# A scan and two expert layers on one core: scatters spaced by steps, one more tile table, later chunks, eight tiles half by half

## The chip, the core and the metric

The kernel runs on one core of one Trainium2 chip. The core has five engines with a queue of instructions each: TensorE (PE; its weight loads are listed as PEld), VectorE (DVE), ScalarE (ACT), GpSimd (POOL) and SyncE (SP), which issues DMAs only. Sixteen DMA engines serve the DMAs of all of them. The metric is the device time of the program in microseconds, the median of several runs.

## The reference

Tokens are 2 x 5056 rows of 256 numbers. A gated scan runs along each sequence; then each token goes through one of eight experts, picked by the largest logit, and the result through a second layer of eight experts with a gate of its own.

```
sig = 1 / (1 + exp(-f_logit)); f = lb + (1 - lb) * sig
h[t] = f[t] * h[t-1] + (1 - f[t]) * x[t]            # y, N = 10112 rows of D = 256
# layer 1: logits = normed(y) @ normed(emb).T / tau;  layer 2: logits = x @ w_gate
e = argmax(logits); g = softmax(logits)[e]
out[n] = g * (relu(x[n] @ w1[e]) @ w2[e])           # w1: 256 x 1024, w2: 1024 x 256, E = 8
```

## The kernel before

**Blocks, chunks, tiles, units.** The 10112 rows are 79 blocks of 128, and a chunk is two blocks (40 chunks, numbered from 0). A chunk is loaded transposed (`p_load`, 512 KB), gated (`p_gate`: tanh on ScalarE, the rest on ScalarE or GpSimd), scanned along the row on VectorE (`p_scan`, L492), transposed on TensorE with its logits (`p_mm`, L507 and L509), scaled and split into a high and a low half of 16 bits (`p_hi`, `p_lo`), and ranked by expert. Two chunks share a row tile of four blocks. GpSimd then scatters each block's 128 rows by an indirect DMA into the table X[0] in DRAM (`p_put`, L638), where every expert has a region of its own.

A tile is 128 rows of one expert. Which expert a tile belongs to and where it starts is computed on the core (`checkpoint`): once the first 16, 32, 48, 64 blocks are scattered, and at the end, a table is made of the tiles that are full by then in any case (9, 16, 16, 16 and the rest). SyncE reads the table into registers and loads a tile with a transposing DMA (`t_load`, L755) and its gate values (L762).

A unit is half an expert for one tile: 512 of the 1024 hidden columns. It has 24 matmuls of 128 columns into PSUM (`mm1`, L780), a Relu on ScalarE and its low part on VectorE (`evac`, L788 and L187, the tile hT) and 12 matmuls of 256 columns (`mm2`, L802). A layer has 83 tiles or 166 units in the main order, 332 units for both; three more tiles of each layer run only if they hold rows. A tile's two units normally follow each other. The first 4 tiles of the kernel (`g0`, group 1) and the last 21 of layer 1 and first 21 of layer 2 (`swap`, group 2) go half by half: all tiles with the first half of the experts, then all with the second, so that the weights of one half can be loaded meanwhile. Such a tile is loaded twice, keeps a partial sum (`o_partial`, L806) and adds it on VectorE (`o_sum`, L195).

**Layer 1 to layer 2.** A finished tile of layer 1 is summed, scaled, split, transposed again (`m_turn`: by DMA for the tiles of group 0 below number 48, on TensorE, L868, for the others), gets its logits, expert and slot (`m_logits` to `m_slot`), and its rows are scattered into X[1] (L948, two scatters for a pair of tiles). Layer 2 reads its tiles from X[1] and scatters its results to the output (L970).

**Weights.** Each expert's half of W1 and of W2 is loaded as 512 KB of 32-bit numbers and split into a high part (`w_hi`, ScalarE) and a low part (`w_lo`, VectorE; four of the first sixteen on TensorE and ScalarE). There are 32 such items for each layer.

**Order.** The order is written out by hand as numbered steps. Step i >= 0 issues unit i; the prologue starts at step -31. Each piece of work is entered at a step with a priority: `at(step, prio, function)`. A chunk c starts at step s0[c]: from -29 in twos, chunk 8 at -9 (`hold`), in twos up to chunk 17 and in fours behind it (`rates`). Its parts follow at fixed distances (`p`): load -2, scan 0, transposes 2, its row tile's four scatters 7 to 10, the checkpoint 7. `m`, `md` and `mg` hold the same for a finished tile (normal, turned by DMA, half by half). Up to step 16 only SyncE keeps this order (`man0`), the other engines' instructions are placed by the framework's scheduler; from step 17 (`mans`) TensorE, SyncE, GpSimd and ScalarE keep it too (`man`). DMAs of chunks and weights go to SyncE ahead of step -6 (`spto`), to ScalarE's queue behind it. Chunks 0 to 7 lie in the buffers of the second half of W2 (`alias`); chunks from 8 on, row tiles and some others share a pool of six buffers (tag `q`). A tile is loaded up to six units ahead (`pre`), into four buffers.

Of the kernel before, what the change touches and what calls it, by code (L numbers as in the profile page):

```python
# [11 lines left out]
I32 = mybir.dt.int32  # L12
# [12 lines left out]

CFG = {'cps': (16, 32, 48, 64),
 'g0': 4,
 'swap': 21,
# [9 lines left out]
 'gdve': 0,  # L38
 'wpe': (4, 0),
 'yg': (0, 0),  # L40
 'man0': ('SP',),
# [6 lines left out]
 'mans': 17,  # L48
 'xtn': 48,
 'md': {'turn': (3, 58),  # L50
        'logits': (8, 3),
# [5 lines left out]
        'up': (12, 45),  # L57
        'done': (12, 57)},
 'hiv': (2,),
# [4 lines left out]
 'sc': (0, 26),  # L64
 'w1': (-8, 0.8),
 'w1s': (20, 0.8),
# [58 lines left out]
def scan_moe_moe_kernel(ctx, tc, xf, emb, cst, tmp, w1a, w2a, w1b, w2b, out, seq, cfg=CFG):  # L125
# [6 lines left out]
    CT = 2  # L132
# [500 lines left out]
    def p_put(q, rows):  # L633
        p = pq[q]
        for i in rows:
            if i >= p["g"]:
                return
            x_write(0, G.indirect_dma_start(out=X[0], out_offset=IndirectOffsetOnAxis(ap=p["sl"][:, i, 0:1], axis=0),  # L638
                                            in_=p["row"][:, i, :].bitcast(I32), in_offset=None, bounds_check=BOUND,
                                            oob_is_err=False))  # L640
            yield
# [72 lines left out]

    ring = {}

    wreg = [T.alloc_register(f"wa{i}") for i in range(16)]
# [66 lines left out]
    def evac(t, h):  # L784
        hps = t.pop("hps")
        hT = hp.tile([P, 8, P], F16, name="hT", tag="hT", bufs=LAG + 2)
        hh = hT.rearrange("p (a c) q -> p a (c q)", a=2)
        A.activation(out=hh[:, 0], in_=hps, func=ACTF.Relu)  # L788
        stt(V, hh[:, 1], hps, 0.0, hh[:, 0], ALU.max, ALU.subtract)
        t["hT", h] = hT  # L790
# [143 lines left out]
    def m_slot(d):  # L934
        g = len(d["t"])
        pz = d["er"]
        assert ranked[1] == 1
        ranked[1] = 0
        tt(V, pz, RK[:, G4:G4 + g], d["oh"][:, 0:g], ALU.mult)
        yield  # L940
        slf = sm.tile([P, CT, 1], F32, name="tslf", tag="tslf")[:, 0:g]
        V.tensor_reduce(out=slf, in_=pz, axis=AX.X, op=ALU.add)
        yield
        sl = sm.tile([P, CT, 1], I32, name="tsl", tag="tsl")[:, 0:g]
        stt(V, sl, slf, 1.0, d["inv"].unsqueeze(2), ALU.mult, ALU.add)
        yield
        for i in range(len(d["t"])):
            x_write(1, G.indirect_dma_start(out=X[1], out_offset=IndirectOffsetOnAxis(ap=sl[:, i, 0:1], axis=0),  # L948
                                            in_=d["row"][:, i].bitcast(I32), in_offset=None, bounds_check=BOUND,
                                            oob_is_err=False))  # L950
            yield

# [94 lines left out]
    for c in range(NCH):  # L1047
        if c == cfg["hold"][0]:
            s = cfg["hold"][1]
        s0[c] = int(s)  # L1050
        s += next(r for n, r in cfg["rates"] if c < n)
    first = min(s0.values())
    for c in range(NCH):
# [8 lines left out]
        if 2 <= c < cfg["alias"]:  # L1062
            at(first - 2 + (c - 2) // 2, 2, p_load, c)
        elif c >= 2:
            pa("load", p_load, c)
        for name, fn in (("gate", p_gate), ("scan", p_scan), ("mm", p_mm), ("sq", p_sq), ("pow", p_pow), ("hi", p_hi), ("lo", p_lo)):
            pa(name, fn, c)
        if c % 2 or c == NCH - 1:
# [7 lines left out]
            else:  # L1076
                for j in range(G4):
                    at(b + j, prio, p_put, q, (j,))

# [110 lines left out]
    def fin_unit(u, i):  # L1190
# [4 lines left out]
        elif h == 1:  # L1195
# [11 lines left out]
            if t["pi"] == len(d["t"]) - 1:  # L1207
                for name, fn in (("scale", m_scale), ("split", m_split), ("turn", m_turn), ("turn2", m_turn2),
                                 ("logits", m_logits), ("top", m_top), ("exp", m_exp), ("rank", m_rank),
                                 ("gat", m_gat), ("slot", m_slot), ("up", m_up), ("done", done_pair)):  # L1210
                    ma(name, fn, d)

    def drain(g):
# [10 lines left out]
    def last_tiles(m):  # L1224
# [22 lines left out]
        with tc.If(n > tl[0]["j"], label=f"tail{m}"):  # L1247
            kept[0] = {}
            assert ranked[1] == 0
            for d in [t["pair"] for t in tl if t["pi"] == 0]:  # L1250
# [9 lines left out]
                for fn in (m_scale, m_split, m_turn, m_turn2, m_logits, m_top, m_exp, m_rank, m_gat, m_slot, m_up):  # L1260
                    drain(fn(d))
                routed[0] += len(d["t"])
            kept[0] = None
# [129 lines left out]
```

## Time and profile before

| what | us |
|---|---|
| median of 3 runs | 1064.48 (1055.07 to 1067.7) |
| the profiled execution | 1052.77 |
| its span, first to last instruction | 1050.9 |
| TensorE busy | 996.1 (95%) |
| VectorE, ScalarE, GpSimd busy | 602.3, 529.2, 407.8 |
| mean granted TensorE clock | 0.985 |

The span is one execution; its own time stands beside it, and it lies below the three timed runs. Busy times are unions of an engine's instructions. A busy TensorE can be waiting inside a matmul or run at half its clock, so its share alone does not tell how near it is to its best.

### The profile page before, as it was taken

How to read it: one execution, taken by the hardware profiler on the slowest of the kernel's cores; microseconds unless marked ns; L12 is line 12 of the kernel's file. 1: busy time of each engine (PE TensorE's matmuls, PEld its weight loads, DVE VectorE, ACT ScalarE, POOL GpSimd, SP SyncE). 2: the span in 40 equal slices, each digit the busy share in tenths (PEclk: the TensorE clock that was granted, in tenths of full speed). 3: DMA queues.
4: the chain of work that ended last, by engine and by line, in shares of the span. 5: the costliest groups of instructions: out<-in, count | busy, mean ns of one | idle time of the engine just before them, and what ended most of it. 6: DMA issues, size and time to landing. Idle time of an engine off the chain costs nothing. (4 is left out here: it accounts for less than half of the span.)

```text
span 1050.9 us, 36737 instructions
## 1 busy us (share of the span) xinstructions
PE 996.1 (95%) x13267; PEld 932.6 (89%) x13267; DVE 602.3 (57%) x1927; ACT 529.2 (50%) x1301; POOL 407.8 (39%) x666
## 2 busy tenths in 40 slices
PE   5557999999999999999999999999999999999997
PEld 4436889999999999999998999999999999999997
DVE  7988877787778777665449778443222222222221
ACT  6978555665655565665346466443333333333332
POOL 5834645666666565332002550243222222222222
PEclk9967999999999999999999999999999999999999
DMA  9798436777677673875479699653322222222220
GB/s 352 244 342 209 132 59 120 144 136 130 124 127 127 152 125 94 195 196 149 62 170 205 123 197 267 117 103 72 52 52 53 52 53 48 45 50 44 47 51 31
DMA packets 195612, 132.69 MB, mean 126 GB/s; under 512 B 169601, under 2 KB 172558, under 8 KB 195440
## 3 DMA queue, kind: packets, MB, share of 16 engines
q1 hardware_dynamic: 172384, 60.18, 29.7%
q10 hardware_dynamic: 11200, 38.62, 14.7%
q0 software_dynamic: 11856, 31.51, 11.7%
q8 instruction: 118, 1.93, 0.8%
q14 instruction: 54, 0.44, 0.2%
HBM read 58.89 MB, written 38.85 MB: 93 GB/s over the span
## 5 line engine op out<-in xcount | busy, mean ns | idle before, releaser
L780 PE MATMUL hps<-xT,W 128*128 128x128 f16 x7968 | 504.9, 220 | 6.9 <-DVE hT L187 3.1
L802 PE MATMUL ops<-W,hT 128*128 x3984 | 489.3, 272 | 1.6 <-ACT acc L806 0.9
L780 PEld LDWEIGHTS <-W 128*128 x7968 | 475.6, 98 | 16.0 <-issue 6.3
L187 DVE SCALAR_TENSOR_TENSOR hT<-hps,hT 128x512 f16<-128x512 f32 x332 | 228.6, 688 | 318.4 <-ACT hT L788 315.7
L802 PEld LDWEIGHTS <-hT 128*128 128x128 f16 x3984 | 374.3, 98 | 41.4 <-issue 2.0
L788 ACT ACTIVATE hT<-hps 128x512 f16<-128x512 f32 x332 | 198.0, 596 | 303.2 <-PE hps L780 284.0
L970 POOL DMA_INDIRECT out<-osum,ti x83 | 81.1, 977 | 291.4 <-ACT osum L966 189.5
L948 POOL DMA_INDIRECT X<-trow,tsl x83 | 97.1, 1170 | 53.2 <-DVE tsl L187 18.0
L638 POOL DMA_INDIRECT X<-row,sl x79 | 92.8, 1174 | 55.1 <-issue 37.7
L966 ACT ACTIVATE osum<-ops,exr 128x256 f32<-128x256 f32 x62 | 29.3, 473 | 47.0 <-PE ops L802 44.8
L195 POOL TENSOR_TENSOR lf<-exr,us 128x2 f32<-128x2 f32 (+1 forms) x42 | 9.7, 231 | 102.6 <-DMA W<-WD 44.0
L187 DVE SCALAR_TENSOR_TENSOR W<-ws,W 128x1024 f16<-128x1024 f32 x34 | 41.5, 1220 | 8.7 <-ACT W L373 8.7
L373 ACT ACTIVATE W<-ws 128x1024 f16<-128x1024 f32 x35 | 37.1, 1060 | 12.5 <-DMA ws<-w2b 8.6
L825 ACT ACTIVATE trow<-osum 128x256 f16<-128x256 f32 x83 | 34.9, 420 | 16.0 <-DMA X<-trow,tsl 7.6
L492 DVE TENSOR_TENSOR_SCAN xf<-xf 128x256 f32<-128x256 f32 (+3 forms) x64 | 42.8, 710 | 0.1
L507 PE MATMUL yt<-cs,xf 128*128 128x128 f32 x126 | 28.3, 303 | 15.2 <-DVE xf L492 10.2
L814 ACT ACTIVATE osum<-ops 128x256 f32<-128x256 f32 x58 | 22.2, 382 | 38.3 <-PE ops L802 38.3
L187 DVE SCALAR_TENSOR_TENSOR trow<-osum,tsc,trow 128x256 f16<-128x256 f32 x83 | 36.7, 481 | 4.1 <-ACT trow L840 3.2
L187 DVE SCALAR_TENSOR_TENSOR xf<-xf 128x512 f32<-128x512 f32 (+1 forms) x32 | 21.8, 681 | 26.7 <-POOL xf L192 19.9
L547 ACT ACTIVATE row<-yt,sc 128x256 f16<-128x256 f32 x79 | 33.5, 481 | 6.5 <-DVE sc L192 6.5
L840 ACT ACTIVATE trow<-osum,tsc 128x256 f16<-128x256 f32 x62 | 28.1, 500 | 16.5 <-DVE tsc L192 14.9
L187 DVE SCALAR_TENSOR_TENSOR row<-yt,sc,row 128x256 f16<-128x256 f32 x79 | 36.0, 472 | 0.2 <-ACT row L547 0.2
(149 smaller groups left out, 929.2 us busy)
## 6 DMA issues: line engine op xcount, KB each, us to landing
xf<-xf ACTq DMA_DIRECT2D x28, 512.0 KB
ws<-w1b ACTq DMA_DIRECT2D x16, 512.0 KB
ws<-w2b ACTq DMA_DIRECT2D x16, 512.0 KB
W<-w1a SPq DMA_DIRECT2D x11, 512.0 KB
W<-xf SPq DMA_DIRECT2D x8, 512.0 KB
ws<-w2a ACTq DMA_DIRECT2D x8, 512.0 KB
WD<-wq SPq DMA_DIRECT2D x8, 512.0 KB
W<-WD SPq DMA_DIRECT2D x8, 512.0 KB
```

The lines of the kernel that those rows point to most:

```text
L187: return eng.scalar_tensor_tensor(out=out, in0=in0, scalar=s, in1=in1, op0=op0, op1=op1, **kw)
L373: A.activation(out=hi, in_=src, func=ACTF.Copy, scale=64.0)
L492: V.tensor_tensor_scan(out=t[:, k, lo:hi], data0=t[:, 2 + k, lo:hi], data1=t[:, k, lo:hi], initial=init, op0=ALU.mult, op1=ALU.subtract)
L547: A.activation(out=p["row"][:, o + i, 0:D], in_=yv(d["yt"][i]), func=ACTF.Copy, scale=p["sc"][:, o + i:o + i + 1])
L638: x_write(0, G.indirect_dma_start(out=X[0], out_offset=IndirectOffsetOnAxis(ap=p["sl"][:, i, 0:1], axis=0), in_=p["row"][:, i, :].bitcast( ...
L780: T.matmul(out=hps[:, c, :], lhsT=w, rhs=xt[:, a, :], start=(n == 0), stop=(n == 5))
L788: A.activation(out=hh[:, 0], in_=hps, func=ACTF.Relu)
L802: T.matmul(out=o, lhsT=hT[:, a + k, :], rhs=w[:, b * D:(b + 1) * D], start=(first and k == 0 and n == 0), stop=(last and k == 3 and n == 2))
L825: A.activation(out=d["row"][:, i, D:2 * D], in_=t["O"], func=ACTF.Square, scale=0.25, accum_out=d["ss"][:, i:i + 1])
L948: x_write(1, G.indirect_dma_start(out=X[1], out_offset=IndirectOffsetOnAxis(ap=sl[:, i, 0:1], axis=0), in_=d["row"][:, i].bitcast(I32), in ...
L966: A.activation(out=r, in_=o, func=ACTF.Copy, scale=ex0[:, 0:1])
L970: i = ins_of(G.indirect_dma_start(out=out, out_offset=IndirectOffsetOnAxis(ap=ti, axis=0), in_=r, in_offset=None, bounds_check=N - 1, oob_ ...
```

## The change

Seven things change together.

- Every scatter of a block or of a layer 1 tile that stands behind step 17 waits for the latest Relu issued so far (`paced`, `evs`). Row scatters there move to the end of their step (`late`, priority 54).
- The two scatters of a finished pair leave `m_slot` and become `m_put`, entered one step apart for tiles that go half by half and two steps apart for the others (`apart`); the count `done` of the tiles turned by DMA follows at 13 instead of 12.
- The tables are made at 16, 24, 32, 48 and 64 blocks (9, 8, 8, 16, 16 tiles and the rest).
- The first eight tiles, not four, go half by half (`g0`). Tiles 4 to 7 so become group 1.
- Chunks 12 to 21 start at steps written out in `first`; before they were -1, 1, 3, 5, 7, 9, 13, 17, 21, 25.
- Chunks 8 to 11 are loaded at steps -18, -17, -12, -10 (`loads`), before at -11, -9, -7, -5; all four so go to SyncE.
- The splitting of layer 1's second half of weights starts at step -4 instead of -8 (`w1`), and with it the loads of its W2.

```diff
--- before.py
+++ after.py
@@ -23,8 +23,8 @@
 RW = 516
 BIG = float(1 << 20)
 
-CFG = {'cps': (16, 32, 48, 64),
- 'g0': 4,
+CFG = {'cps': (16, 24, 32, 48, 64),
+ 'g0': 8,
  'swap': 21,
  'cp2': 65,
  'lag': 3,
@@ -37,6 +37,8 @@
  'urgent': ('scan', 'mm', 'sq', 'pow', 'hi', 'norm', 'top', 'rank', 'rec', 'exp', 'slot', 'up', 'gat', 'put', 'cp'),
  'gdve': 0,
  'wpe': (4, 0),
+ 'first': {12: 0, 13: 2, 14: 5, 15: 8, 16: 11, 17: 14, 18: 17, 19: 19, 20: 22, 21: 25},
+ 'loads': {8: -18, 9: -17, 10: -12, 11: -10},
  'yg': (0, 0),
  'man0': ('SP',),
  'wa': 3,
@@ -47,6 +49,8 @@
  'alias': 8,
  'mans': 17,
  'xtn': 48,
+ 'apart': (2, 1),
+ 'late': 54,
  'md': {'turn': (3, 58),
         'logits': (8, 3),
         'top': (8, 51),
@@ -55,14 +59,14 @@
         'rank': (10, 46),
         'slot': (11, 13),
         'up': (12, 45),
-        'done': (12, 57)},
+        'done': (13, 57)},
  'hiv': (2,),
  'y1': 'V',
  'wg': (0, 0, 0, 0),
  'whv': 0,
  'spto': -6,
  'sc': (0, 26),
- 'w1': (-8, 0.8),
+ 'w1': (-4, 0.8),
  'w1s': (20, 0.8),
  'w2': (-2, 1.15),
  'pre1': (-19, 2.2),
@@ -635,9 +639,9 @@
         for i in rows:
             if i >= p["g"]:
                 return
-            x_write(0, G.indirect_dma_start(out=X[0], out_offset=IndirectOffsetOnAxis(ap=p["sl"][:, i, 0:1], axis=0),
-                                            in_=p["row"][:, i, :].bitcast(I32), in_offset=None, bounds_check=BOUND,
-                                            oob_is_err=False))
+            x_write(0, paced(G.indirect_dma_start(out=X[0], out_offset=IndirectOffsetOnAxis(ap=p["sl"][:, i, 0:1], axis=0),
+                                                  in_=p["row"][:, i, :].bitcast(I32), in_offset=None, bounds_check=BOUND,
+                                                  oob_is_err=False)))
             yield
 
 
@@ -713,6 +717,13 @@
 
 
     ring = {}
+    evs = []
+
+    def paced(i):
+        if now[0] > cfg["mans"] and not inside[0]:
+            tc.add_manual_dep(ins_of(i), evs[-1].name, mybir.DependencyInfo(mybir.DependencyClass.Sync, mybir.DependencyReason.DATA),
+                              reason="one step apart")
+        return i
 
     wreg = [T.alloc_register(f"wa{i}") for i in range(16)]
     vreg = [T.alloc_register(f"va{i}") for i in range(4)]
@@ -785,7 +796,7 @@
         hps = t.pop("hps")
         hT = hp.tile([P, 8, P], F16, name="hT", tag="hT", bufs=LAG + 2)
         hh = hT.rearrange("p (a c) q -> p a (c q)", a=2)
-        A.activation(out=hh[:, 0], in_=hps, func=ACTF.Relu)
+        evs.append(ins_of(A.activation(out=hh[:, 0], in_=hps, func=ACTF.Relu)))
         stt(V, hh[:, 1], hps, 0.0, hh[:, 0], ALU.max, ALU.subtract)
         t["hT", h] = hT
 
@@ -943,12 +954,13 @@
         yield
         sl = sm.tile([P, CT, 1], I32, name="tsl", tag="tsl")[:, 0:g]
         stt(V, sl, slf, 1.0, d["inv"].unsqueeze(2), ALU.mult, ALU.add)
-        yield
-        for i in range(len(d["t"])):
-            x_write(1, G.indirect_dma_start(out=X[1], out_offset=IndirectOffsetOnAxis(ap=sl[:, i, 0:1], axis=0),
-                                            in_=d["row"][:, i].bitcast(I32), in_offset=None, bounds_check=BOUND,
-                                            oob_is_err=False))
-            yield
+        d["sl"] = sl
+
+    def m_put(d, i):
+        if i < len(d["t"]):
+            x_write(1, paced(G.indirect_dma_start(out=X[1], out_offset=IndirectOffsetOnAxis(ap=d["sl"][:, i, 0:1], axis=0),
+                                                  in_=d["row"][:, i].bitcast(I32), in_offset=None, bounds_check=BOUND,
+                                                  oob_is_err=False)))
 
     def m_up(d):
         rank_up(1, d["oh"], CT)
@@ -1047,7 +1059,7 @@
     for c in range(NCH):
         if c == cfg["hold"][0]:
             s = cfg["hold"][1]
-        s0[c] = int(s)
+        s0[c] = cfg["first"].get(c, int(s))
         s += next(r for n, r in cfg["rates"] if c < n)
     first = min(s0.values())
     for c in range(NCH):
@@ -1061,6 +1073,8 @@
 
         if 2 <= c < cfg["alias"]:
             at(first - 2 + (c - 2) // 2, 2, p_load, c)
+        elif c in cfg["loads"]:
+            at(cfg["loads"][c], 2, p_load, c)
         elif c >= 2:
             pa("load", p_load, c)
         for name, fn in (("gate", p_gate), ("scan", p_scan), ("mm", p_mm), ("sq", p_sq), ("pow", p_pow), ("hi", p_hi), ("lo", p_lo)):
@@ -1075,7 +1089,7 @@
                 at(b, prio, first_of_all(p_put) if c < cfg["cps"][0] // CT else p_put, q, range(G4))
             else:
                 for j in range(G4):
-                    at(b + j, prio, p_put, q, (j,))
+                    at(b + j, prio if b < cfg["mans"] else cfg["late"], p_put, q, (j,))
 
             def cp0(q):
                 for m, cnt, n, fin, key in cpl:
@@ -1209,6 +1223,8 @@
                                  ("logits", m_logits), ("top", m_top), ("exp", m_exp), ("rank", m_rank),
                                  ("gat", m_gat), ("slot", m_slot), ("up", m_up), ("done", done_pair)):
                     ma(name, fn, d)
+                for j in range(CT):
+                    at(i + MO["slot"][0] + cfg["apart"][bool(t["grp"])] * j, 40 if MO["slot"][1] < 40 else 55, m_put, d, j)
 
     def drain(g):
         for _ in g or ():
@@ -1259,6 +1275,8 @@
                     m_sq(t)
                 for fn in (m_scale, m_split, m_turn, m_turn2, m_logits, m_top, m_exp, m_rank, m_gat, m_slot, m_up):
                     drain(fn(d))
+                for j in range(CT):
+                    m_put(d, j)
                 routed[0] += len(d["t"])
             kept[0] = None
         inside[0] = False
```

## Rows read from the trace of the kernel before

**Rows 1.** The page, part 1: busy time, share of the span, instructions.

```profile
PE 996.1 (95%) x13267; PEld 932.6 (89%) x13267; DVE 602.3 (57%) x1927; ACT 529.2 (50%) x1301; POOL 407.8 (39%) x666
```

**Rows 2.** Timeline of ScalarE: the Relu of single units, early and late.

```profile
150.76 0.60 ACT L788 ACTIVATE hT<-hps 128x512 f16<-128x512 f32 x1 [1.30 <-PE RK L431]
...
400.47 0.60 ACT L788 ACTIVATE hT<-hps 128x512 f16<-128x512 f32 x1 [1.13 <-PE hps L780]
...
790.39 0.60 ACT L788 ACTIVATE hT<-hps 128x512 f16<-128x512 f32 x1 [0.87 <-PE hps L780]
793.04 0.60 ACT L788 ACTIVATE hT<-hps 128x512 f16<-128x512 f32 x1 [2.05 <-PE hps L780]
```

**Rows 3.** Windows: length; busy time (instructions) per engine; granted clock; DMA share; GB/s.

```profile
0.00:26.00 26.00, 13.34 (x69) 11.80 (x69) 20.22 (x72) 16.86 (x49) 15.16 (x28) 1.00 0.94 352
26.00:53.00 27.00, 16.01 (x77) 11.38 (x75) 24.59 (x92) 24.46 (x59) 22.26 (x17) 1.00 0.75 248
53.00:79.00 26.00, 14.64 (x56) 9.27 (x56) 21.05 (x40) 19.64 (x44) 9.10 (x10) 0.64 1.00 340
0.00:82.77 82.77, 46.54 (x212) 34.69 (x212) 69.60 (x206) 64.73 (x158) 46.52 (x54) 0.86 0.86 302
82.77:106.34 23.57, 17.30 (x177) 15.76 (x178) 20.90 (x48) 18.71 (x49) 13.05 (x12) 0.83 0.86 220
106.34:150.76 44.42, 42.21 (x540) 38.94 (x540) 35.45 (x136) 24.86 (x84) 23.68 (x34) 1.00 0.40 103
150.76:190.17 39.41, 39.40 (x547) 37.42 (x546) 27.90 (x106) 23.42 (x71) 22.31 (x37) 1.00 0.67 113
190.17:400.00 209.83, 209.83 (x2963) 200.27 (x2961) 163.06 (x641) 126.01 (x389) 130.42 (x216) 1.00 0.70 131
400.00:660.00 260.00, 256.11 (x3637) 241.12 (x3635) 174.32 (x626) 143.03 (x323) 74.62 (x150) 1.00 0.77 169
```

**Rows 4.** Timeline of TensorE, 72 to 110 us: start, length, line, tiles, [idle before].

```profile
80.23 1.07 PE L507 MATMUL yt<-cs,xf 128*128 128x128 f32 x3 [1.59 <-ACT row L547]
...
82.77 5.06 PE L780 MATMUL hps<-xT,W 128*128 128x128 f16 x48
...
88.95 1.65 PE L780 MATMUL hps<-xT,W 128*128 128x128 f16 x24
...
94.94 2.72 PE L780 MATMUL hps<-xT,W 128*128 128x128 f16 x24 [3.07 <-DVE hT L187]
```

**Rows 5.** Timeline of GpSimd, 26 to 60 us: row scatters.

```profile
34.02 1.87 POOL L638 DMA_INDIRECT X<-row,sl  x1 [0.30 <-issue]
...
43.01 1.38 POOL L638 DMA_INDIRECT X<-row,sl  x1 [0.30 <-issue]
...
56.70 3.23 POOL L638 DMA_INDIRECT X<-row,sl  x1 [0.30 <-issue]
```

**Rows 6.** Timeline of SyncE's queue, 12 to 76 us: DMA issues.

```profile
27.48 18.18 SPq L360 DMA_DIRECT2D W<-w2a  x4
45.71 0.42 SPq L451 DMA_DIRECT2D xf<-xf  x1
...
47.14 0.67 SPq L451 DMA_DIRECT2D xf<-xf  x1
...
65.49 1.31 SPq L755 DMA_TRANSPOSE xT<-X  x1
```

**Rows 7.** Groups by form, whole run: count, busy us, mean ns of one, idle before.

```profile
L187 DVE SCALAR_TENSOR_TENSOR W<-ws,W 128x1024 f16<-128x1024 f32 x34 | 41.5, 1220 | 8.7 <-ACT W L373 8.7
...
L195 DVE TENSOR_TENSOR osum<-ops,acc 128x256 f32<-128x256 f32 x46 | 19.4, 421 | 0.6 <-PE ops L802 0.6
...
L868 PE MATMUL x2p<-id,trow 128*128 128x128 f16 x156 | 12.4, 219 | 1.9 <-DVE hT L187 1.3 <-DVE wq L187 0.3 <-PEq L1247 0.3
```

**Rows 8.** Timeline of VectorE at the first table: its widest instruction.

```profile
50.26 0.23 DVE L195 TENSOR_TENSOR le<-ct,cs 128x72 f32<-128x72 f32 x1
```

## The prediction, made before the run

> **What bounds the kernel now.** I read the busy table of the page first, then windows cut at the points where TensorE changes its behaviour, then the timelines of single engines around the first matmul unit, and last the groups by form for prices. TensorE is busy for 996.1 of the span's 1050.9 us [rows 1], but a busy TensorE need not run at its rate, so what counts is the pace of the units. In the late part one Relu follows another by 2.65 us [rows 2] and nothing else is in the way; 332 units at that pace are 880 us. From 150.76 us on TensorE shows hardly a gap: 39.40 busy of 39.41 us, then 209.83 of 209.83, then 256.11 of 260 [rows 3]. What the kernel can lose or win there without a change in TensorE's own work is the last of these, 3.9 us, and the little there is before it. What is left is the beginning. The first unit starts at 82.77 us [rows 4], and in the 23.57 us after it TensorE is busy for only 17.30, at a mean granted clock of 0.83 [rows 3]; since the two levels are 0.5 and 1, a third of that stretch, 8.0 us, ran at 1.2 GHz and could have cost up to half of itself. So the ramp behind the first unit loses 6.3 us of idle time and at most 4.0 of slow clock. The end of the kernel is therefore the start of unit 0, plus the ramp's loss, plus an amount of TensorE work that the change hardly touches.
>
> **What holds unit 0 back.** Its rows are ready earlier. The sixteenth row scatter, the last that the first tile table needs, is issued at 56.70 us [rows 5], and the first transposing load of a tile goes out at 65.49 [rows 6]. On TensorE, whose order ahead of step 17 is the scheduler's, the transposes of chunk 11 stand directly ahead of unit 0, at 80.23 [rows 4]. Chunks 8 and 9 are loaded only at 45.71 and 47.14, because SP's queue stood still between the first and the last of four weight loads, 27.48 to 45.66 [rows 6]; in that stretch the DMA engines moved 248 GB/s, against 352 before and 340 behind it [rows 3]. VectorE was busy for 69.60 of the first 82.77 us, or 84% [rows 3]. So two things hold the start: late chunk data, and a VectorE that is nearly full.
>
> **The change, part by part.**
>
> Eight tiles half by half, and the W1 shift from -8 to -4. Units 0 to 7 now need the first half of each expert alone, so the second half's weights are due four units later, and the code moves their splitting by four steps. Of that, the eight low parts of W1 (half 1) cross from the steps before unit 0 to steps -1 to 4. One costs 1.22 us of VectorE [rows 7], eight 9.8 us. The loads themselves aren't moved (steps of their own), except those of W2's second half, eight loads four steps later. VectorE's work ahead of unit 0 becomes 69.60 - 9.8 = 59.8 us; at the share of 84% it is done at 71.2 us. The load of the first tile at 65.49 sets a floor near it: the landing isn't shown, I bound it by 1.3 us (its issue) and 17 (unit 0 itself), and take 5, nearer to the issue, since the next ones leave SP within 5 us. I take a start at 72.3, so 10.5 us are gained; from 70 to 82.77 is open.
>
> Chunks 8 to 11 loaded at steps -18, -17, -12, -10. In SP's order the first two go ahead of the weight load that stood still, so they leave near 12 to 15 us, thirty earlier. Moving them costs the weights behind them 2 x 0.52 MB / 352 GB/s = 3.0 us [rows 3]; what hides this is SP's later standstill of 18 us. Chunks 10 and 11 each take a buffer of the pool of six that a row tile leaves, by the order of allocation those of the first and the second row tile, whose last scatters are at 34.02 and 43.01 [rows 5]; the weight loads behind them went out from 45.71 on [rows 6], so nothing is pushed by more than 1 to 2 us. This part has no term of its own: it makes the 72.3 possible. The Trainium skill (DMA: Bandwidth & Descriptors, Issuing engines are not separate DMA queues) says that loads from several engines share the same DMA engines and that the choice of the engine saves issue time alone. By that rule the 3.0 us would be paid in full by the weights, and the sum below would be 3.0 us later; the row with 248 GB/s says that there is room, so I don't charge it.
>
> Chunks 12 to 21 later. Chunk 17 goes from step 9 to 14, chunk 21 stays at 25. Up to step 29 both kernels have done the same chunks, so TensorE's total up to there is equal; in between the load on VectorE is thinner. With a chunk go its load of 0.52 MB on ScalarE's queue, its gate on POOL and its two row scatters; ahead of step 29 none of them passes another chunk's, so each queue keeps its order. Term: 0.
>
> One more table, at 24 blocks. It lets the chunks come later without starving unit 18. Its price is some 22 small VectorE instructions of at most 0.23 us [rows 8], 5.1 us at most, on an engine that isn't the bound after the ramp; no term for TensorE.
>
> Four more tiles with a partial sum. Tiles 4 to 7 are now turned on TensorE and not by DMA: 12.4 us / 39 tiles = 0.32 us each [rows 7], 1.3 us in all, on the path. Their partial sums add some 0.42 us per tile on VectorE, 1.7 us (hidden), and four more loads of a tile on SP.
>
> Spaced scatters. Each step now holds at most one scatter of a tile, and POOL waits at it for the Relu of a unit that has just been issued; behind it in POOL's order stand the gate operations of the next chunk and the small products of the routing, and for those VectorE waits. But those need ScalarE's results of the same or the next step, which stand behind that Relu on ScalarE anyway. POOL is busy for 130.42 of 209.83 us in the even stretch [rows 3]. I take 0, with bounds of -3.9 us (all gaps of the stretch up to 660 go) and +17 (below). "done" at step 13 only follows the second scatter.
>
> **Sum.** -10.5 + 1.3 = -9.2 us. On the profiled execution, 1052.77 us (span 1050.9 and 1.9 around it), that gives 1043.6. The timed runs have their median at 1064.48, 11.7 above the profiled one, so the forecast is 1064.48 - 9.2 = 1055.3.
>
> A check on VectorE: up to unit 29, at 190.17 us, it was busy for 69.60 + 20.90 + 35.45 + 27.90 = 153.85 us [rows 3]. The change adds 5.1 + 1.7, so 160.6 must fit. At 181 us that is 89%; the fullest stretch of the trace is 24.59 of 27 us, 91% [rows 3]. So the gain can be had, but not much more: at 91% unit 29 comes at 176.5, and 13.7 us is the most.
>
> **Rivals.**
>
> *The start doesn't move, or VectorE takes it back.* If the scheduler again puts a late chunk ahead of unit 0, or if VectorE runs at 84% as before the first unit, 160.6 us of work end at 191.2, one us later than now. Time: 1064.48 + 1.0 + 1.3, about 1066. For it: sixteen low parts now fall between units -1 and 10. Against it: VectorE has long waits in the old ramp that came from bunched chunks.
>
> *The slow clock stays.* Unit 3's 24 matmuls took 2.72 us at half the clock [rows 4], against 1.65 for unit 2's at the full one. If all eight first units run so, 8 x 1.07 = 8.6 us are given back: 1064.48 - 9.2 + 8.6 = 1063.9. The rows show the low level where TensorE was often idle, a mean of 0.64 between 53 and 79 us with 14.64 of 26 us busy [rows 3]. The Trainium skill (TensorE: Matmul & The Clock Gate, HAM oscillation — how this bites in real kernels) says that waits between bursts of matmuls throttle the clock again; by that rule half-fed units keep it low, and the trace agrees with its 0.64. Against it: units without second-half weights have less to wait for.
>
> *More than the start.* If the ramp's loss shrinks with it (to the VectorE limit, 13.7 us) and the 11.7 us by which timed runs exceed the profiled one were stalls behind bunched scatters, the time is 1064.48 - 13.7 - 11.7 = 1039. For it: the spread of the timed runs, 12.6 us. Against it: no scatter ends a wait of TensorE in this trace, whose gaps behind 150.76 are 3.9 us.
>
> *POOL becomes the bound (slower).* In the stretch from 190.17 to 400 us POOL has 79.4 us idle [rows 3], and by the code about one scatter per step; the steps there take (400.47 - 150.76) / 82 = 3.05 us [rows 2], so 69 scatters. A hold of more than 1.15 us at each fills POOL. A wait for the Relu of the same step, half a step or 1.4 us on average (between 2.65 and 3.05 a step), would do so: (1.4 - 1.15) x 69 = 17 us, less 9.2: 1072.
>
> **How the numbers follow.** Forecast (1048 to 1060) 0.43; start unmoved 0.22; slow clock 0.08; more 0.13; POOL 0.14. The range runs from 1037 (the rival of more, and the gaps) to 1073 (POOL's). Two per cent, about what a measurement of this kernel can tell from no change, is 21.3 us: below 1043.2 only the third rival reaches, with 0.09 of its 0.13; above 1085.8 POOL's price would have to be doubled, 0.04.
>
> **What would show it.** Right: the first unit's matmuls near 72 us, with chunk 11's transposes before 70; chunks 8 and 9 issued by SP before 20 us; VectorE near 89% up to unit 29, and unit 29's Relu near 181; after it the same pace as now. Wrong: a first unit that still starts past 80, units 0 to 10 at over 4.5 us each, a granted clock of 0.5 in them, or waits of VectorE for POOL that grow after unit 17.

## The result and the profile after

Measured side by side, the changed kernel takes 1073.34 us (median of 20 runs, 1063.94 to 1079.89) and the kernel before 1064.52 (20 runs, 1055.07 to 1070.58): a ratio of 1.0092 [1.0068, 1.0115]. It is slower, by less than 2%, where 1055.3 was forecast. Timed again beside later experiments (e16 below) it stood at 1.0069 [1.0038, 1.0100]. Its profiled execution took 1073.68 us, with a span of 1071.9. The profiled execution of before, 1052.77, lies below all of these 20 runs of before, so from the two traces alone the loss looks twice as large as it is (21.0 us of span); sizes below come from ratios, places from traces.

The page of the changed kernel, part 1, as in [rows 1]:

```profile
PE 1003.4 (94%) x13283; PEld 933.5 (87%) x13283; DVE 601.2 (56%) x1952; ACT 526.0 (49%) x1305; POOL 404.0 (38%) x666
```

Windows of it (columns as in [rows 3]), up to unit 0, the ramp, the even stretch, and two around the branch of layer 1's tail:

```profile
0.00:81.96 81.96, 46.49 (x212) 33.98 (x213) 69.09 (x206) 64.86 (x164) 44.30 (x54) 0.82 0.89 300
81.96:105.00 23.04, 18.73 (x206) 16.72 (x207) 19.46 (x55) 16.85 (x41) 10.74 (x12) 0.87 1.04 219
190.00:400.00 210.00, 209.24 (x2931) 198.70 (x2929) 161.56 (x638) 122.84 (x384) 124.99 (x215) 1.00 0.66 128
460.00:470.00 10.00, 9.34 (x139) 8.75 (x136) 7.41 (x23) 6.23 (x13) 2.01 (x6) 1.00 0.65 188
470.00:480.00 10.00, 6.75 (x75) 6.00 (x76) 2.36 (x6) 3.30 (x7) 1.74 (x2) 0.83 0.35 96
```

The forecast's first sign is missing: VectorE has 69.09 us of work ahead of unit 0, where 69.60 stood in [rows 3] and 59.8 was expected. Its TensorE timeline at unit 0 and at the tail, against [rows 4]:

```profile
78.06 0.69 PE L511 MATMUL yt<-cs,xf 128*128 128x128 f32 x2 [2.09 <-DVE row L191]
...
81.96 6.41 PE L791 MATMUL hps<-xT,W 128*128 128x128 f16 x69 [0.49 <-ACT lg L531]
...
473.25 1.01 PE L879 MATMUL x2p<-id,trow 128*128 128x128 f16 x8 [3.91 <-PEq L1263]
```

Unit 0 starts at 81.96 (82.77 before), with chunk 11's transposes again right ahead of it. The same queue of SyncE and scatters of GpSimd, against [rows 6] and [rows 5]:

```profile
14.05 0.33 SPq L455 DMA_DIRECT2D xf<-xf  x1
...
16.57 0.33 SPq L455 DMA_DIRECT2D xf<-xf  x1
...
40.44 0.33 SPq L455 DMA_DIRECT2D xf<-xf  x1
...
49.42 0.33 SPq L455 DMA_DIRECT2D xf<-xf  x1
...
67.11 1.31 SPq L766 DMA_TRANSPOSE xT<-X  x1
```

```profile
53.47 1.10 POOL L642 DMA_INDIRECT X<-row,sl  x1 [8.15 <-DVE row L634]
...
63.28 1.96 POOL L642 DMA_INDIRECT X<-row,sl  x1 [0.30 <-issue]
```

Chunks 8 and 9 are loaded thirty microseconds earlier, as forecast. But the sixteenth scatter goes out 6.6 us later (63.28 against 56.70) and the first tile's load 1.6 us later.

Followed by units, the loss has two places. Against before's profile the changed kernel is 7.0 us ahead at unit 15 and level at unit 30 (-0.3); behind by 2.7 at unit 120 and by 7.6 at unit 124; then by 7.7 at unit 156 and 20.7 at unit 196, and by the same to the end. Its second profile (e16) loses in the same two places, 5.8 us from unit 120 to 124 and 12.6 from unit 156 to 196, though it is 6.5 us ahead at unit 30. A second profile of before (e4) is itself 4.2 behind at unit 124 and 7.0 at the end, so a difference of that size between two traces proves nothing by itself; the experiments decide.

### The profile page after: what moved, and what is told of

Same layout as the page of the kernel before. It is cut to its first block, busy times and chain, and to the rows that moved or that the text cites. A ratio compares the mean times of both kernels' runs of the same rounds, so it can differ in the third digit from the quotient of the medians.

```text
span 1071.9 us, 36861 instructions
## 1 busy us (share of the span) xinstructions
PE 1003.4 (94%) x13283; PEld 933.5 (87%) x13283; DVE 601.2 (56%) x1952; ACT 526.0 (49%) x1305; POOL 404.0 (38%) x666
## 5 line engine op out<-in xcount | busy, mean ns | idle before, releaser
L791 PEld LDWEIGHTS <-W 128*128 x7968 | 474.9, 98 | 27.6 <-issue 10.6
L961 POOL DMA_INDIRECT X<-trow,tsl x83 | 94.2, 1135 | 58.0 <-DVE hT L191 18.5
L642 POOL DMA_INDIRECT X<-row,sl x79 | 88.0, 1114 | 62.0 <-issue 17.5
L836 ACT ACTIVATE trow<-osum 128x256 f16<-128x256 f32 x83 | 34.9, 421 | 30.7 <-DMA X<-trow,tsl 21.9
L511 PE MATMUL yt<-cs,xf 128*128 128x128 f32 x126 | 27.6, 299 | 11.6 <-issue 9.2
L851 ACT ACTIVATE trow<-osum,tsc 128x256 f16<-128x256 f32 x62 | 28.1, 500 | 20.9 <-DVE tsc L196 13.6
L199 POOL TENSOR_TENSOR ri<-ss,hf 128x4 f32<-128x4 f32 (+1 forms) x20 | 25.0, 1252 | 29.6 <-ACT lg L531 28.7
L513 PEld LDWEIGHTS yt<-cs,xf 128*128 128x128 f32 x252 | 35.6, 204 | 0.0
```

What stands on the lines that cost most here:

```text
L199: return eng.tensor_tensor(out=out, in0=in0, in1=in1, op=op)
L513: T.matmul(out=yt[:, D:D + E], lhsT=t[:, k, i * P:(i + 1) * P], rhs=ide[:, (1 - k) * (P + E):(1 - k) * (P + E) + E], start=(k == 0), stop= ...
L642: x_write(0, paced(G.indirect_dma_start(out=X[0], out_offset=IndirectOffsetOnAxis(ap=p["sl"][:, i, 0:1], axis=0), in_=p["row"][:, i, :].bi ...
L791: T.matmul(out=hps[:, c, :], lhsT=w, rhs=xt[:, a, :], start=(n == 0), stop=(n == 5))
L836: A.activation(out=d["row"][:, i, D:2 * D], in_=t["O"], func=ACTF.Square, scale=0.25, accum_out=d["ss"][:, i:i + 1])
L961: x_write(1, paced(G.indirect_dma_start(out=X[1], out_offset=IndirectOffsetOnAxis(ap=d["sl"][:, i, 0:1], axis=0), in_=d["row"][:, i].bitca ...
```

## The experiments

Two theories at the start: S, the spaced and held scatters cost the time; E, the early half (table at 24, later chunks, eight tiles half by half, early loads, W1 shift) does. All ratios are to the kernel before, on the same chip in the same session.

| run | what it is | median us (runs) | ratio [95%] |
|---|---|---|---|
| e1 | before + early half | 1073.02 (6) | 1.0112 [1.0087, 1.0136] |
| e2 | before + scatter half | 1071.41 (6) | 1.0087 [1.0066, 1.0109] |
| e3 | whole change, scatters not held | 1076.83 (6) | 1.0135 [1.0105, 1.0164] |
| e15 | before + only the last pairs spaced and held | 1068.79 (6) | 1.0103 [1.0056, 1.0150] |
| e11, e11b | scatter half, last pairs together | 1059.73, 1062.97 (12, 12) | 0.9977 [0.9946, 1.0007], 0.9990 [0.9963, 1.0017] |
| e5 | whole change, last pairs together | 1067.84 (10) | 1.0060 [1.0027, 1.0093] |
| e6b | whole change, branch a unit earlier | 1065.88 (12) | 1.0031 [0.9999, 1.0063] |
| e14 | early half, branch a unit earlier | 1069.70 (11) | 1.0055 [1.0029, 1.0081] |
| e10, e10b | whole change, both edits | 1057.61, 1052.15 (12, 9) | 0.9959 [0.9928, 0.9989], 0.9923 [0.9884, 0.9961] |
| e9 | e5 + low parts behind unit 0 | 1067.57 (10) | 1.0034 [0.9995, 1.0072] |
| e13 | e10 + low parts behind unit 0 | 1055.72 (12) | 0.9961 [0.9932, 0.9989] |
| e12 | before + low parts behind unit 0 | 1069.02 (12) | 1.0051 [1.0023, 1.0080] |
| e16 | the changed kernel again | 1065.46 (12) | 1.0069 [1.0038, 1.0100] |

### The halves

e1 takes from the diff `cps`, `g0`, `first`, `loads`, `w1` and the two lines that read `first` and `loads`; e2 takes all the rest; e3 is the changed kernel with the hold off:

```diff
     def paced(i):
-        if now[0] > cfg["mans"] and not inside[0]:
+        if False:
```

> Only the early half of the change: eight tiles half by half, the table at 24 blocks, chunks 12 to 21 later, chunks 8 to 11 loaded earlier, W1 from step -4. The scatters are as before, without spacing or hold. Theory S (the spaced scatters cost the time, in the passage from layer 1 to layer 2, where ScalarE and SyncE wait for them): equal to before or up to 8 us faster, a ratio of 0.993 to 1.002, and the pace of units 150 to 190 as before. Theory E (the early half costs it: the first table comes later and the later chunks are paid back on TensorE): the whole 8.8 us are here, a ratio of 1.006 to 1.010.

> Only the scatter half: row scatters at the end of their step, pair scatters one or two steps apart, each held for the latest Relu, and the count at step 13; the start is that of the kernel before. Theory S: 1.006 to 1.012, with the loss between units 150 and 190, where layer 2's first tiles are loaded. Theory E: 0.997 to 1.002.

> The whole change without the hold: the scatters stand where the change puts them but wait for no Relu. Theory S with the hold as the cost (GpSimd waits for the Relu and everything behind it is late): back to 1.000 or below. Theory S with the place as the cost (scatters one step apart and last in their step land later): stays at 1.006 to 1.010. Theory E: stays at 1.006 to 1.010 too, and only the run with the early half alone tells it from the second.

> The kernel before once more, for a second profile: its first one, 1052.8 us, lies below all of its timed runs. If the timed runs' excess of 12 us is stalls in the passage between the layers (DMA load of 1.1 to 1.2 there), this profile shows gaps of TensorE between 550 and 680 us that the first did not have; if it is in the start, unit 16's Relu comes later than 150.8 us.

Each half alone costs as much as the whole (1.0112, 1.0087, 1.0092), so S and E were each half right and the costs don't add up; and e3 shows that the hold isn't the price: without it the time is no better. e4, one execution of before, took 1059.62 us; of its 7.0 us over the first profile 4.1 arise between units 30 and 120 and 3.2 between units 156 and 196 (TensorE idle for 5.5 us there, against 3.0), and its unit 16, at 149.26, is no later. What the halves do by themselves had to be looked for place by place.

### Pairs at the passage from layer 1 to layer 2

e5 lets the two scatters of a pair of group 2 (the last 21 tiles of layer 1) leave together and unheld; e11 does so to the scatter half; e15 spaces and holds these pairs alone, on the kernel before (it keeps `m_put` and the count at 13, which e11 has too). Beside the lines shown, `m_put` leaves out the hold for these pairs in e5 and e11 and has it for them alone in e15.

```diff
-                    at(i + MO["slot"][0] + cfg["apart"][bool(t["grp"])] * j, ..., m_put, d, j)
+                    far = 0 if t["grp"] == 2 else cfg["apart"][bool(t["grp"])]
+                    at(i + MO["slot"][0] + far * j, ..., m_put, d, j)
```

> The changed kernel with one part of it taken back: the row scatters of the pairs of the last group of tiles before layer 2 are issued together again and wait for no Relu; everything else stays as changed. Theory S2 (the spaced, held scatters cost in the passage from layer 1 to layer 2, because the table of layer 2 lands later, X tiles load later and TensorE waits for them): units 156 to 196 come back by 7 to 9 us, ratio to the kernel before 1.000 to 1.004, span about 1063. Theory B (the loss is mostly elsewhere, in the branch and the low clock behind it): under 3 us come back, ratio above 1.006.

> The kernel before with the scatter half of the change, but the pairs of the last group together and not held, so that what is left is the spaced and held row scatters of the first layer and of the earlier pairs. Theory S2 (the passage is the scatter half's whole cost): ratio 0.998 to 1.003, against 1.009 with the pairs spaced. Theory R (holding scatters for a Relu costs in the first layer too): ratio above 1.005, with units 0 to 120 later than before by more than 3 us.

> The kernel before with only the spaced and held row scatters of the first layer and the earlier pairs, timed again beside the other half. Ratio 0.995 to 1.001 if its first time stands; then the two halves without their two losses are each about even and e10's 0.992 to 0.996 is what they give together.

> The kernel before with one edit alone: the second scatter of each pair of the last group one unit later, and both held for a Relu. Theory S2 (this is the scatter half's whole cost): ratio 1.006 to 1.011, X tiles of layer 2 waited for between units 180 and 196. Theory R (the first layer's spaced scatters cost as well, or instead): ratio under 1.004.

Spacing these pairs alone makes 1.0103, and the scatter half without it is even (0.9977, 0.9990): S holds, and within intervals of 0.3% this is all of it. Where: ScalarE's timeline in e16, and TensorE's beside it (both the changed kernel):

```profile
582.16 1.08 ACT L887 ACTIVATE x<-x2p 128x512 f16<-128x512 f16 x2
588.88 0.42 ACT L836 ACTIVATE trow<-osum 128x256 f16<-128x256 f32 x1 [5.64 <-DMA X<-trow,tsl]
589.20 0.19 ACT L836 ACTIVATION_READ_ACCUMULATOR trow<-osum 128x1 f32 x1
589.29 0.58 ACT L799 ACTIVATE hT<-hps 128x512 f16<-128x512 f32 x1
```

```profile
591.03 1.50 PE L791 MATMUL hps<-xT,W 128*128 128x128 f16 x24 [2.90 <-DVE ter L191]
```

The Square at L836 writes into a row tile `trow`, which is free only when both scatters of an older pair have landed. With the second scatter a unit later it waits, here for 5.64 us; the Relu of the running unit stands behind it on ScalarE (589.29), VectorE's low part behind that, and TensorE stops. The waits of that one line, summed over the passage by the view of waits, in e16, e15, e10b and e11b:

```profile
ACT trow L836 <- DMA X<-trow,tsl: 26.1, 6, 5.6
```

```profile
ACT trow L834 <- DMA X<-trow,tsl: 26.8, 6, 6.2
```

```profile
ACT trow L836 <- DMA X<-trow,tsl: 8.5, 4, 3.2
```

```profile
ACT trow L834 <- DMA X<-trow,tsl: 2.1, 2, 1.6
```

In all eight profiles with spaced pairs this sum is 20.1 to 27.6 us, e3 without hold included (21.6); in the others, before among them (7.6), it is 0.4 to 8.5. The length of the passage itself, from unit 156's Relu to unit 196's, separates the two groups less well: 121.3 to 130.2 us in the eight, 127.0 on average, and 117.2 to 126.6 in the other twelve, 121.1 on average, so some 6 us by the traces. What TensorE loses, windows of the passage in e16, e10b and e15:

```profile
564.87:694.63 129.76, 116.13 (x1630) 107.92 (x1628) 83.86 (x296) 65.02 (x142) 45.09 (x76) 1.00 0.78 156
```

```profile
562.01:681.36 119.35, 114.21 (x1630) 107.62 (x1628) 85.00 (x296) 66.24 (x143) 42.91 (x77) 1.00 0.86 177
```

```profile
564.11:689.08 124.97, 116.09 (x1630) 108.05 (x1629) 84.30 (x296) 65.85 (x142) 43.47 (x77) 1.00 0.78 165
```

The same 1630 matmuls at the full clock; idle time 13.6 us with the change, 5.1 with the pairs together. In e16 7.1 us of it are waits for the X tiles of layer 2 (4.2 in the first profile of the changed kernel), in e10b 1.5; the last pair's scatter stands 75.4 us behind unit 156's Relu, against 68.4 in e10b. In e15 the idle time is 8.9 us, where before has 3.0 in the same units; only 0.6 of it is a wait for X tiles, which had been expected there, and 6.7 end with instructions of VectorE. So the wait on ScalarE costs time without late X tiles, and in the changed kernel late X tiles come on top. No run gives the row tiles more buffers, which would show how much of the loss the buffer alone makes. e5 fell short of its forecast in the ratio: in its trace 10.9 us of the passage are back (units 156 to 196 lose 2.1 us to before's profile, in the changed kernel 13.0), in the ratio only 3.2 thousandths, with an interval of about as much on either side. The clearer comparison is within one session, with the branch of the next part moved in both: e10, pairs together, stands at 0.9959, against 1.0031 for e6b, pairs spaced, some 7.6 us.

### The branch of layer 1's tail

The three spare tiles of layer 1 run only if they hold rows; the `If` of `last_tiles(0)` decides it on every engine, three units ahead of the first tile of group 2. e6 and e6b move it, and the register read that it needs, one unit earlier, and leave everything else; e10 is e5 with that, e14 is e1 with that, e16 is the changed kernel again.

```diff
- 't0at': (-3, 40),
+ 't0at': (-4, 40),
```

> The changed kernel with the branch around the tail of layer 1's first table, and the register read that it rests on, one unit earlier. Theory P (the 4.3 us branch on TensorE comes from where the branch falls in the instruction stream): the branch takes 0.4 us again, no TensorE gap of 3.9 us and no stretch of low clock behind it, units 120 to 124 about 5 us shorter than in the changed kernel. Theory Q (it waits on something that the early half makes late): 4 us again, at whichever unit.

> The changed kernel with only the branch of layer 1's tail one unit earlier, now timed. Theory P (the branch costs 4.3 us on TensorE plus a low clock behind it, whatever else the run does): ratio to the kernel before 1.002 to 1.006, that is 4 to 7 us below the changed kernel. Theory N (its one look was a lucky execution, and the loss lies elsewhere): ratio 1.007 to 1.011, like the changed kernel.

> The changed kernel with both edits: the last group's pair scatters together and not held, and the branch one unit earlier. If the two losses are separate (passage and branch) the sum of both comes back: ratio 0.996 to 1.001, no TensorE gap behind the branch, units 156 to 196 within 5 us of the kernel before. If they share one cause, or the loss lies elsewhere, ratio above 1.003.

> The changed kernel with the last group's pair scatters together and the branch one unit earlier, timed again, as the partner of the next run. If its first time was no accident: ratio 0.993 to 0.999.

> The kernel before with the early half of the change alone (the new table, the later chunks 12 to 21, the loads of chunks 8 to 11) and the branch of layer 1's tail one unit earlier. Theory P (the branch is the early half's cost, 6 of its 12 us, and the rest is TensorE starved in units 18 to 27 because the row scatters come there in bunches): ratio 1.003 to 1.007, TensorE still waits at units 18 to 27. Theory Q (the branch is the whole cost of the early half): ratio 0.997 to 1.002.

> The changed kernel itself, on the same chip as the others and with a second profile. Ratio 1.007 to 1.011 as before; the branch of layer 1's tail takes 3.9 to 4.4 us again if that belongs to the program, 0.4 if it belonged to the execution.

TensorE's queue at the `If`, from the view of that line (count: shortest/median/longest in ns, first and last start), in before, in the changed kernel, in e16 and in e10b:

```profile
L1247 PEldq COMPARE_BRANCH  x1: 429/429/429, 465.9 to 465.9; - x1
```

```profile
L1263 PEldq COMPARE_BRANCH  x1: 4312/4312/4312, 468.6 to 468.6; - x1
```

```profile
L1263 PEldq COMPARE_BRANCH  x1: 4879/4879/4879, 460.6 to 460.6; - x1
```

```profile
L1265 PEldq COMPARE_BRANCH  x1: 429/429/429, 460.2 to 460.2; - x1
```

It belongs to the program, not to the execution: 3.87 to 4.88 us in all seven profiles that have the early half with the branch at its old place, 0.43 or 0.44 in all seven without the early half, and 0.42 to 0.52 in all six with the early half and the branch a unit earlier. Behind the long branch TensorE falls to 1.2 GHz for a moment: the window 470 to 480 above has a granted clock of 0.83. From unit 120's Relu to unit 124's it is 15.0 to 18.1 us in the seven profiles with the long branch and 11.8 to 12.4 in the thirteen others. e6, one execution, took 1059.39 us; timed, e6b stands at 1.0031, 0.004 to 0.006 below the changed kernel, and both edits together (e10, e10b) are below the kernel before. The passage was expected to stay within 5 us of before's in e10; its profiled execution, 1071.29 us where the median is 1057.61, was 9.0 longer there, e10b's 2.2.

The Trainium skill (Runtime: NRT & Kernel Launch, Instruction fetch mechanics) says that instructions are read ahead in sequence in blocks of 16 KiB, and that a taken branch to a place outside what is held makes the engine fetch the target first. The trace agrees as far as it goes: inside e16's 4.88 us the DMA view lists exactly one packet of an instruction queue, of 0.02 MB, and moving the code by one unit ends the wait. Over the whole execution that queue, q8, moved one packet more in the changed kernel than in e10b (DMA part of the pages: packets, MB, share; the changed kernel first):

```profile
q8 instruction: 119, 1.95, 0.8%
```

```profile
q8 instruction: 118, 1.93, 0.9%
```

It is 119 in all seven profiles with the long branch and 118 in all thirteen others. So one more fetch of instructions goes with the long branch each time. Which engine's queue q8 is, the view doesn't tell, so the mechanism is likely and not shown to the end.

e14 answers what the early half costs otherwise: 1.0055. TensorE's timeline in units 20 to 28 of it:

```profile
168.94 1.28 PE L782 MATMUL hps<-xT,W 128*128 128x128 f16 x20 [1.18 <-issue]
...
181.05 0.71 PE L804 MATMUL ops<-W,hT 128*128 x5 [1.16 <-issue]
...
195.50 0.49 PE L782 MATMUL hps<-xT,W 128*128 128x128 f16 x6 [1.08 <-issue]
```

TensorE stops in the middle of a unit's matmuls, for nothing that the profile shows ("issue"): 5.8 us in nine such waits between 158 and 196 us. In e1 the same happens between units 20 and 28 (5.1 us in ten waits). In e10b and e16, with the scatters placed apart, there is none in that stretch, and e3, placed apart but not held, has one of 0.7 us, so it isn't the hold that ends the stops. So the scatter half without the last pairs earns its place beside the early half, where two row scatters and a pair's two would leave as four, 1.3 us apart; alone it is even. That the bunches cause the stops is not shown: the kernel before has six scatters 1.3 to 2.0 us apart between 154 and 162 us, and TensorE is busy for 39.40 of 39.41 us there [rows 3]. Why it stops without a wait stays open.

### The start of unit 0

e7 loads chunks 8 to 11 at the old steps (`'loads': {}`). e9 (on e5), e13 (on e10) and e12 (on the kernel before) do what the forecast thought the change would do: the low parts of W1's second half wait for unit 0's own low part.

```diff
-                with tc.issue_after(tablast[0]):
+                with tc.issue_after(lows[0] if lows and i <= 24 else tablast[0]):
```

> The changed kernel with chunks 8 to 11 loaded at the old steps. Theory L (chunk 8's work, loaded early, stands between GpSimd's first table and its reciprocal and holds the 16th row scatter back): the 16th scatter returns from 63.3 us to 57 to 60, the first X tile is loaded by 66, unit 0 starts no later than 82. Theory V (VectorE's low parts of the weights hold unit 0): the scatters come earlier but unit 0 still starts at 81 to 83 us, with 69 to 70 us of VectorE work ahead of it.

> The kernel of e5 with the eight low parts of W1's second half tied behind unit 0's own low part, so that they cannot be placed ahead of it. Theory V (VectorE's low parts hold the start, which is what the forecast had assumed the change does): unit 0 starts 7 to 9 us earlier, at 73 to 75 us, VectorE has about 60 us of work ahead of it, and the time is 5 to 9 us below e5's. Theory D (the start is set by the first table and chunk 11, not by these parts): unit 0 stays within 2 us of 82 and the time within 2 us of e5's, or the parts come back as waits of VectorE in units 0 to 30.

> The kernel before with one edit: the low parts of W1's second half that it issues up to the 24th are tied behind unit 0's own low part. It tests the forecast's chain alone, without the rest of the change. Forecast's chain (the end follows the start of unit 0): unit 0 starts some 5 to 10 us earlier and the time falls by as much, ratio 0.990 to 0.996. Theory D (TensorE's chunk work and the clock set unit 30, whenever unit 0 starts): unit 0 starts earlier, but unit 30 stays within 2 us and the ratio is 0.998 to 1.004.

> The same kernel with the low parts of W1's second half tied behind unit 0's own low part. Forecast's chain (the end follows the start of unit 0): unit 0 starts near 75 us and the ratio falls by 5 to 7 us against its partner, to 0.989 to 0.992. Theory D (units 0 to 30 take the earlier start back, in TensorE's chunk work and its clock): unit 0 near 75 us, unit 30 within 2 us of the partner, ratio within 0.003 of the partner's.

e7 brings the sixteenth scatter back to 55.8 us and the first tile's load to 64.9, and unit 0 still starts at 82.89; it took 1079.41 us, in one execution. So not the table, but VectorE holds unit 0: before and after the change it does 21 and 22 low parts ahead of it. In e9 and e13 it does 13, and unit 0 starts at 75.20 and 76.62. Yet the time doesn't follow: e13 is at 0.9961 where its partner e10b is at 0.9923. Windows of e13 and, behind it, of e10b:

```profile
90.00:110.00 20.00, 11.94 (x93) 9.69 (x92) 20.00 (x37) 13.26 (x29) 7.09 (x7) 0.76 0.70 168
```

```profile
90.00:110.00 20.00, 17.81 (x186) 15.46 (x185) 19.02 (x59) 14.09 (x39) 8.09 (x7) 0.91 0.89 194
```

VectorE's timeline in e13 says why:

```profile
86.07 0.68 DVE L191 SCALAR_TENSOR_TENSOR hT<-hps,hT 128x512 f16<-128x512 f32 x1
86.67 8.02 DVE L191 SCALAR_TENSOR_TENSOR W<-W,W 128x1024 f16<-128x1024 f32 x7
```

Seven low parts stand in one block right behind unit 0's, the next units wait, VectorE is busy for 20.00 of 20 us and TensorE for 11.94, at a clock of 0.76. Unit 30's Relu comes at 194.16, against 188.11 in e10b, though unit 0 was 4.6 us earlier. Two profiles of the changed kernel differ by as much at that unit (192.60, and 186.38 in e16), so how much later it is, one pair of traces can't say. That the earlier start is not kept, a second pair shows too: e9 against e5, unit 0 at 75.20 against 79.14, unit 30 at 193.50 against 189.36, VectorE busy for 20.00 of the same 20 us, and the medians within 0.3 us. e13 was expected within 0.003 of its partner if the ramp takes the start back; it is 0.0038 above, and the 5 to 7 us of the other theory are not there. In e12 the edit didn't reach its aim: 20 low parts still ran ahead of unit 0, against 21, it started at 82.42, and the time rose. It tells nothing of the chain.

## Why the prediction was wrong

**What it got right.** Chunks 8 and 9 left SyncE at 14.05 and 16.57. The even stretch kept its pace: 209.24 of 210.00 us busy, against [rows 3], with GpSimd no fuller (124.99 us against 130.42 in nearly the same stretch), so the rival of a full GpSimd fell, though its sign was right. Four more tiles cost 1.2 us on TensorE (x172 for 13.6 us, against x156 for 12.4 in [rows 7]); 1.3 was the term. The early loads, though, which had no term, sent the sixteenth scatter out 6.6 us later.

**The term of -10.5 us failed.** "... the eight low parts of W1 (half 1) cross from the steps before unit 0 to steps -1 to 4." They didn't: ahead of step 17 VectorE's order is the scheduler's, and the only tie of these parts is to the first table's last instruction. The steps say where the work is entered, not where it runs; 22 low parts still ran ahead of unit 0. The prediction had stated that rule for TensorE and not applied it to VectorE. "The start doesn't move" was the rival at 0.22, and unit 29's Relu came at 190.86, where that rival had 191.2 and the forecast 181. That it fits so closely is in part luck: in e16, the same kernel, unit 0 started at 80.46 and unit 29's Relu came at 183.43. The start stayed in both; what the ramp loses behind it differs by 6 us from one execution to the next.

**And the step under it failed too.** "The end of the kernel is therefore the start of unit 0, plus the ramp's loss, plus an amount of TensorE work that the change hardly touches." e13 moved the start by 4.6 us and e9 by 3.9, and neither got faster than its partner beyond the noise. The terms aren't independent: work that leaves VectorE ahead of unit 0 is due right behind it, where VectorE is full (20.00 of 20 us), and the ramp's loss grows by what the start gains. That is the second half of the same rival, "VectorE takes it back".

**The 0 for the spaced scatters failed.** The bound of +17 was priced at GpSimd filling up in layer 1. What they cost stands at the passage: 1% or some 11 us in e15 (the interval is 6 to 16), some 7.6 us between e6b and e10. A scatter that leaves later keeps a row tile, and ScalarE waits for the buffer. The argument looked for scatters that end a wait of TensorE and found none; it didn't follow them one engine further, to ScalarE, which in the trace of before already waits 7.6 us for them at L825. Its windows also end at 660 us [rows 3], inside the passage, which runs from 564.55 to 681.74 in before.

**What it didn't have at all** is the branch: 4 us and a low clock behind it. The trace of before shows 0.43 us and nothing that it could be ten times as long. It missed a gain as well: beside the early half, the rest of the scatter half ends TensorE's stops (units 16 to 30 take 56.7 us in e14 and 48.3 in e10b; the ratios differ by 0.010 and 0.013 between e14 and e10 and e10b, across sessions).

**What adds up and what doesn't.** Branch and pairs taken out together bring the change from 1.0092 and 1.0069 to 0.9959 and 0.9923, some 14 us (13.3 between e16 and e10b, in one session); taken out singly they bring 1 to 3 (e5) and 4 to 6 us (e6b) with intervals of about 3 each. Whether the sum is larger than its parts these intervals can't tell, and it stays open. The version that beats both kernels is e10.

## What to carry to other kernels

Ask of every transfer that is made later which buffer it holds and which in-order engine will next write there: the price appears at that engine's queue, not at the issuer. A start that comes earlier is worth what the fullest engine behind it can still take, so look at that engine's share in the stretch right after, before the start becomes a term. And where steps are only hints to a scheduler, read from the trace what stood ahead of the event before taking work out of the sum.

## What was not expected of the hardware

- The same branch on TensorE's queue took 0.42 to 0.52 us or 3.87 to 4.88, by where the code around it lies, and one packet more of an instruction queue goes with the long one (119 against 118, in 20 of 20 profiles); VectorE's, ScalarE's and SyncE's took 0.05 to 0.07 in the same trace.
- TensorE can stop for 0.2 to 1.2 us in the middle of a row of matmuls with nothing to wait for in the profile (5.8 us in e14, none in e10b, where the scatters stand further apart; before has a bunch of six and no stop).
- An early load moved other work: with chunks 8 and 9 loaded at 14 and 17 us GpSimd's ninth scatter waited 8.15 us for VectorE's reciprocal, and the sixteenth went out 6.6 us later; with the old loads (e7) it went out at 55.80.
